# Attention beside a gated feed-forward layer: value products of two chunks together, row maxima eight blocks ahead, one ring of queries and keys

## The chip, the cores and the metric

The kernel runs on one core of a Trainium2 chip. A core has five engines, each with an instruction queue of its own that is worked through in order: PE (matmuls, with its weight loads shown as PEld), DVE (vector), ACT (scalar: exponentials, copies, casts), POOL (general purpose) and SP, which here issues nearly all DMA transfers. The metric is the device time of one execution in microseconds (us). Before the change it is 826.45 us, the median of 3 runs (826.08 to 826.83).

## The reference

Input x has 2048 rows of 512. The output is `g * a + (1 - g) * b` with `g = sigmoid(sum(x * gate_w))` per row. `b` is a feed-forward layer, `(silu(x @ w_gate) * (x @ w_up)) @ w_down` with 1792 hidden columns. `a` is attention with 32 heads of 16 columns and a window of 256:

```python
scores = jnp.einsum("bhqd,bhkd->bhqk", q, k) * (Dh ** -0.5)
mask = (idx[:, None] - idx[None, :] >= 0) & (idx[:, None] - idx[None, :] < W)
p = _softmax(jnp.where(mask[None, None], scores, -1e9), axis=-1)
o = jnp.einsum("bhqk,bhkd->bhqd", p, v)
```

All of it is float32. The kernel gets near that with a fast matmul type (F32R) by splitting each operand into a high and a low part, with three products (high-high, high-low, low-high) in place of one.

## The kernel before

**Blocks, chunks, groups.** The 2048 rows are 16 blocks of 128, or 4 chunks of 512. Eight groups `g` have four heads each; a group's heads are worked on as two pairs (`pr`), and the two heads of a pair lie in the lower and upper 64 partitions of one tile.

**Queries and keys.** `proj` or, in the main loop, a unit `("p", g)` computes a group's queries and keys. ACT copies the result out of PSUM, ACT casts the high part and POOL subtracts for the low part (`split_qk`, whose subtraction stands on the helper's line 68), into a tile pair `X`. Then `stack` (lines 242 to 248) writes rows of X into the tiles `QT` and `KT`: for each pair and each of three combinations of high and low parts one DMA for the queries and one for the keys, 12 in all, from SBUF to SBUF. A call moves half a sequence (1024 columns, 128 KB a DMA). There are two sets of QT and KT (`QT[g % 2]`): one group's scores are computed from one set while the next group's fill the other.

**Stage 1, stage 2, value products.** `stage1` (line 251) multiplies a block of queries with up to three blocks of keys on PE (line 263), and DVE adds the mask and takes each row's maximum (line 265). `put_max` (line 272) turns a half's maxima on DVE and writes them to DRAM in one DMA; `get_max` (line 278) brings them back in four DMAs as row 63 or 127 of the query tiles. The keys hold -1 there, so the second product comes out with the maximum taken off. `stage2` (line 293) computes the transposed scores on PE (line 304), ACT takes exponentials into tiles `pt` (line 306), and POOL zeroes what the window leaves out (lines 308, 311). `av` (line 316) multiplies a chunk's `pt` with the values, which `load_v` (line 288) has brought from DRAM: 96 matmuls (64 for chunk 0) in 64-by-32 tiles of the array (line 328), against 64-by-128 tiles everywhere else in the main loop. One PSUM bank of pool `pp` and one of `ps2` hold the two halves of the sum. `finish` (line 333) adds the halves, normalizes and sends the chunk to DRAM in five steps, with a DMA on POOL's queue.

**The main loop** (line 601) has 128 slots `t` (group `t // 16`, block `t % 16`) and one more. A slot has four steps (`hd` in the code). Each step puts into PE's queue one stage-1 product of the next group, one stage-2 product of this group and six matmuls of a unit (line 215). A unit takes four slots: the product of x with a 128-column part of a feed-forward weight (kept in DRAM as `raws`, lines 519 and 522) or the queries and keys of a later group. In the last group there is no stage 1. In the first of every four slots (`part == 0`), at step 1, one `av` follows, then `finish` begins. `later(t, hd, ...)` sets other work to a slot and step: `prepare` in step 3 of a unit's first slot splits the next weight (ACT, then POOL on line 68) and lets SP fetch the one after it (line 73). There is one buffer for a raw weight, so that fetch waits in SP's queue until POOL has read the last one. Nothing plans the order: each engine's queue is what the code writes, and SP's queue stands still behind a DMA that waits.

**Ahead of the loop**, x and the first weights are split, four value blocks and the first groups' queries and keys are computed, and stage 1 of group 0 (16 blocks) runs among the value products of the remaining blocks. **Behind it** comes the feed-forward part (`step`, `hidden`), whose first tiles come from `raws`, and the attention's output product.

Of the kernel before, what the change touches and what calls it, by code (L numbers as in the profile page):

```python
# [9 lines left out]
F32 = mybir.dt.float32  # L10
# [6 lines left out]
P = 128  # L17
# [11 lines left out]
EV = 5  # L29
# [4 lines left out]
def gated_mix(ctx, tc, xT, xn, w01, wqk, wv, wo, wgu, wd, gw, out):  # L34
# [14 lines left out]
    mxd = dram.tile([2 * G, P, 32], F32, name="mxd")  # L49
# [57 lines left out]
    QT = [[slot(f"q0{pr}") for pr in range(2)]]  # L107
    KT = [[slot(f"k0{pr}") for pr in range(2)]]
# [26 lines left out]
    for g in range(2, G):  # L135
        UNITS += early[:2] + [("p", g)] + early[2:3]
        early = early[3:]
# [20 lines left out]
    def load_wd(f, piece, raw=None, engs=dve):  # L158

        WD[f] = halves_of(piece)  # L160
        raw = fetch(wd[f], raw)
        return lambda: split(*WD[f], raw, *engs)
# [6 lines left out]
    with ExitStack() as A:  # L169
# [14 lines left out]
        def x_pair(pool=None, name="x"):  # L184
            return tuple((pool or sm).tile([P, 2 * CH], F32R, name=f"{name}{w}", bufs=1) for w in ("hi", "lo"))

        def split_qk(g, hf, cc, raw, los=nc.gpsimd):
            hi, lo = (t[:, cc * CH:(cc + 1) * CH] for t in X[g, hf])
            split(hi, lo, raw, nc.scalar, los)
# [40 lines left out]
        def proj(g, c, pool, name, todo=None, los=nc.gpsimd):  # L230

            hf, cc = divmod(c, 2)
            if cc == 0:
                X[g, hf] = x_pair() if g == hf else x_pair(vpool, f"x{g}{hf}")

            def done(ps):
                raw = kept()
                nc.scalar.copy(raw, ps)
                split_qk(g, hf, cc, raw, los)
# [10 lines left out]
        MX = {}  # L250
        def stage1(g, qb):

            hf, b = divmod(qb, NB // 2)
            if b == 0:
                MX[g, hf] = sm.tile([P, 4, NB // 2], F32, name="mx")
            q0, k0 = qb * P, max(0, qb - 2) * P
            n = q0 + P - k0
            for hd in range(4):
                pr, j = divmod(hd, 2)
                r = slice(64 * j, 64 * j + 63)  # L260

                ps = ps2.tile([P, CH], F32, name="ps2") if g == 0 and pr else ps1.tile([P, CH], F32, name="ps1")
                nc.tensor.matmul(ps[:, :n], QT[g % 2][pr][r, q0:q0 + P], KT[g % 2][pr][r, k0:k0 + n],  # L263
                                 start=True, stop=True)
                mx = nc.vector.tensor_tensor_reduce(out=ps[:, :n], in0=ps[:, :n], in1=mask[:, 3 * P - n:],  # L265
                                                    scale=1.0, scalar=NEG, op0=ALU.add, op1=ALU.max,
                                                    accum_out=MX[g, hf][:, hd, b:b + 1])
                if g == 0:
                    BEHIND.append(mx)
                yield  # L270

        def put_max(g, hf):
            mt = sm.tile([P, 32], F32, name="mt")
            nc.vector.transpose(mt, MX[g, hf].rearrange("p h b -> p (h b)"))
            u = 2 * g + hf
            nc.sync.dma_start(mxd[u], mt)

        def get_max(g, hf):
            v = mxd[2 * g + hf].rearrange("(q h b) e -> h b q e", q=4, h=4)
            for pr in range(2):  # L280
                q = halves_of(QT[g % 2][pr])[hf]
                for j in range(2):
                    nc.sync.dma_start(q[64 * j + 63:64 * j + 64].bitcast(F32).rearrange("p (b q e) -> p b q e", b=NB // 2, q=4),
# [9 lines left out]
        def stage2(g, kb):  # L293
# [4 lines left out]
            for hd in (1, 0, 3, 2):  # L298
# [4 lines left out]
                ps = ps1.tile([P, CH], F32, name="ps1") if g == G - 1 and pr else ps2.tile([P, CH], F32, name="ps2")  # L303
                nc.tensor.matmul(ps[:, :n], KT[g % 2][pr][r, k0:k0 + P], QT[g % 2][pr][r, k0:k0 + n],  # L304
# [11 lines left out]
        def av(g, c):  # L316


            AV[g, c] = (pp.tile([P, CH], F32, name="pb" if 4 * g + c + 1 < len(UNITS) else "pa"),
# [13 lines left out]
        def finish(g, c):  # L333


            first, second = AV[g, c]
            both = osb.tile([P, CH], F32, name="on")
            lo = 0 if c else 64
            nc.scalar.copy(both[:, lo:], second[:, lo:])
            yield  # L340
            nc.vector.tensor_tensor(out=both[:, lo:], in0=first[:, lo:], in1=both[:, lo:], op=ALU.add)
            if lo:
                nc.vector.tensor_copy(both[:, :lo], first[:, :lo])
            yield
            ot = osb.tile([P, CH], F32, name="on")
            nc.vector.transpose(ot, both)
            yield
            v = ot.rearrange("p (s e) -> p s e", e=32)
            rc = osb.tile([P, CH // 32], F32, name="rc", bufs=1)
            nc.vector.reciprocal(rc, v[:, :, DH])  # L350
            nc.vector.tensor_tensor(out=v[:, :, :DH], in0=v[:, :, :DH],
                                    in1=rc[:, :, None].to_broadcast([P, CH // 32, DH]), op=ALU.mult)
            yield
            on = osb.tile([P, CH], F32, name="on")
            nc.vector.transpose(on, ot)
            nc.gpsimd.dma_start(od[g, :, c * CH:(c + 1) * CH], on)
            yield
# [19 lines left out]

        fill_rows(QT[0], 0.0, 0, nc.vector)

# [35 lines left out]
        xraw = [h for w in "qk" for pr in range(2) for h in halves_of(slot(f"{w}1{pr}", F32))]  # L415
        xraw = [halves_of(h) for h in xraw]
        xraw = [[xraw[2 * c + k // 2][k % 2] for k in range(NK)] for c in range(NCH)]
# [27 lines left out]
        fill_rows(KT[0], -1.0, 0, nc.gpsimd)  # L445
        make_mask()
        split_w(0, nc.vector)
# [4 lines left out]
        fill_rows(QT[0], 0.0, 1, nc.gpsimd)  # L452
        fill_rows(KT[0], -1.0, 1, nc.gpsimd)
        run(vproj(0))
        split_x(1, range(2, NK))
        run(vproj(1))
        split_x(2, range(2))
        run(vproj(2))
        split_x(2, range(2, NK))
        run(proj(0, 1, pp, "pa", los=nc.vector))  # L460
        stack(0, 0)
        run(vproj(3))
        run(proj(1, 1, pp, "pa"))
        split_x(3)
        QT.append([slot(f"q1{pr}") for pr in range(2)])
        KT.append([slot(f"k1{pr}") for pr in range(2)])
        for c in range(2, NCH):
            run(proj(0, c, pp, "pa", los=nc.vector))
        for hf in range(2):
            fill_rows(QT[1], 0.0, hf, nc.gpsimd)  # L470
            fill_rows(KT[1], -1.0, hf, nc.gpsimd)
        stack(0, 1)
        send_v(1)
        send_v(3)
        stack(1, 0)


        first = chain(*(stage1(0, b) for b in range(NB)))
# [5 lines left out]
        for n, turn in enumerate(turns):  # L484
            for m, _ in enumerate(turn, 3 * NK * n):
                run(first, 2 * (2 * NB * max(m + 1 - 8, 0) // (total - 8) - 2 * NB * max(m - 8, 0) // (total - 8)))
            if n == 3:
                prepare()
            if n == 8:
                put_max(0, 0)  # L490
            if n == 9:
                get_max(0, 0)
        run(first)
        for c in range(2, NCH):
# [5 lines left out]
        ptp = A.enter_context(tc.tile_pool(name="ptp", bufs=13))  # L500
        osb = A.enter_context(tc.tile_pool(name="osb", bufs=2))
# [7 lines left out]
        def unit(key, t):  # L509
# [4 lines left out]
            def done(hf):  # L514
                def copies(ps):
                    t0 = t + 3 + hf
                    places = [kept(), kept()]
                    for m in range(2):
                        later(t0, 2 * m, lambda m=m: nc.scalar.copy(places[m], ps[m]))  # L519
# [296 lines left out]
```

## Time and profile before

| | |
|---|---|
| median of 3 runs | 826.45 us (826.08 to 826.83) |
| profiled execution, its own time | 825.82 us |
| its span, first to last instruction | 824.1 us |
| granted PE clock, share of full | 0.999 |
| busy: PE / PEld / DVE / ACT / POOL | 99% / 82% / 62% / 55% / 42% |
| mean DMA rate | 162 GB/s |
| DMAs that SP issues for `stack` / `put_max` / `get_max` | 192 / 16 / 64 |

The profile is of one execution, 0.63 us under the median of the runs; the span leaves out 1.7 us of it. PE is called busy while any matmul is in flight, so its 99% doesn't say that it runs at its best rate: the start times of its matmuls say that. In a timeline row stand the start, the time taken, engine, line, operation, output and inputs with their shape, and in brackets the idle time before it and what ended that. SPq is the queue of SP. "x2" joins two instructions.

### The profile page before, as it was taken

To read this page: it belongs to the slowest core of one execution; us is meant where nothing else is said; L and a number is where in the kernel's file an instruction comes from. 1 tells how busy PE (TensorE), PEld (TensorE's weight loads), DVE (VectorE), ACT (ScalarE), POOL (GpSimd) and SP (SyncE) were. 2 spreads that over 40 slices of the span, in tenths; PEclk is the share of its full clock that TensorE was granted. 3 is DMA by queue.
4 is the path that set the end of the run, shared out by engine and by line. 5 is a ranking of instruction groups with operands and counts; after the bars stand their busy time and mean duration, and the time that the engine had idled before them with its cause. 6 is when DMAs were issued, how large, how long until landed. Compare 5 with 4: busy or idle time off the path is not lost.

```text
span 824.1 us, 21565 instructions
## 1 busy us (share of the span) xinstructions
PE 815.9 (99%) x8306; PEld 677.6 (82%) x8306; DVE 509.8 (62%) x1422; ACT 451.6 (55%) x940; POOL 343.1 (42%) x631
## 2 busy tenths in 40 slices
PE   9999999999999999999999999999999999999998
PEld 6788988888888988887888888877778888888886
DVE  5496677677667676676677677745548443443443
ACT  6422666666666666666666666666647423334341
POOL 5812555555546555555554654456600111011020
PEclk9999999999999999999999999999999999999999
DMA  8484525625634643642652553556769444573621
GB/s 293 111 259 148 167 101 156 180 96 139 195 109 115 188 135 98 183 143 90 181 167 88 172 157 114 147 190 226 248 224 371 158 156 123 165 218 102 213 94 51
DMA packets 70582, 133.27 MB, mean 162 GB/s; under 512 B 14288, under 2 KB 19024, under 8 KB 70480
## 3 DMA queue, kind: packets, MB, share of 16 engines
q1 hardware_dynamic: 66512, 118.00, 46.4%
q0 software_dynamic: 3968, 13.90, 4.6%
q8 instruction: 65, 1.06, 0.5%
q14 instruction: 37, 0.30, 0.1%
HBM read 61.08 MB, written 45.61 MB: 129 GB/s over the span
## 4 chain that ended last, share of the span: by engine, by line
PE 88%; DMA 4%; POOL 3%; DVE 2%; SPq 1%; ACT 1%; issue 1%; ACTq 0%; POOLq 0%
PE pb L215 22%; PE pa L215 22%; PE pb L328 7%; PE ps L263 6%; PE ps L85 6%; PE ps L84 6%; PE ps L83 6%; PE ps L304 4%; PE pb L84 2%; PE pb L85 2%; PE pb L83 2%; PE ps L328 2%; DMA ev<-wd 1%; PE pb L708 1%; PE pa L708 1%
## 5 line engine op out<-in xcount | busy, mean ns | idle before, releaser
L265 DVE CUSTOM_DVE_ANT_0 ps<-ps,mask 128x384 f32<-128x384 f32 (+2 forms) x512 | 272.2, 540 | 142.5 <-PE ps L263 76.8
L306 ACT ACTIVATE pt<-ps 128x384 f32<-128x384 f32 (+2 forms) x512 | 240.8, 477 | 114.9 <-PE ps L263 56.8
L308 POOL TENSOR_SCALAR_AFFINE_SELECT pt<-pt 128x256 f32<-128x256 f32 x256 | 108.2, 423 | 212.5 <-ACT pt L306 204.0
L304 PE MATMUL ps<-q,k 64*128 64x384 f32 (+2 forms) x512 | 162.5, 328 | 0.0
L263 PE MATMUL ps<-k,q 63*128 63x384 f32 (+2 forms) x512 | 158.6, 330 | 0.0
L215 PE MATMUL pb<-xhi,wh 64*128 64x512 f32 x512 | 115.2, 394 | 0.0
L215 PE MATMUL pb<-xlo,wh 64*128 64x512 f32 x512 | 114.0, 391 | 0.0
L215 PE MATMUL pb<-xhi,wl 64*128 64x512 f32 x512 | 113.8, 392 | 0.0
L215 PE MATMUL pa<-xhi,wh 64*128 64x512 f32 x512 | 112.3, 393 | 0.0
L215 PE MATMUL pa<-xlo,wh 64*128 64x512 f32 x512 | 110.9, 391 | 0.0
L215 PE MATMUL pa<-xhi,wl 64*128 64x512 f32 x512 | 110.7, 391 | 0.0
L263 PEld LDWEIGHTS ps<-k,q 63*128 63x128 f32 x512 | 88.8, 185 | 16.1 <-issue 5.4
L311 POOL TENSOR_SCALAR_AFFINE_SELECT pt<-pt 128x256 f32<-128x256 f32 x224 | 98.7, 441 | 0.0
L304 PEld LDWEIGHTS ps<-q,k 64*128 64x128 f32 x512 | 93.0, 185 | 5.6 <-issue 0.8
L712 DVE TENSOR_TENSOR sg<-got,sg 128x512 f32<-128x512 f32 x50 | 44.5, 889 | 51.4 <-ACT sg L711 48.1
L328 PE MATMUL ps<-pt,vg 64*32 64x320 f32 (+4 forms) x1408 | 75.2, 346 | 0.0
L328 PE MATMUL pb<-pt,vg 64*32 64x320 f32 (+3 forms) x1360 | 74.0, 350 | 0.8 <-ACT ev L519 0.7
L265 DVE DVE_READ_ACCUMULATOR2_ANT mx<- 128x1 f32 x512 | 72.1, 141 | 0.0
L328 PEld LDWEIGHTS pb<-pt,vg 64*32 64x32 f32 x1360 | 46.5, 106 | 29.1 <-ACT pt L306 9.9
L215 PEld LDWEIGHTS pb<-xhi,wh 64*128 64x128 f32 x512 | 59.3, 185 | 8.6 <-ACT ev L519 0.3
L215 PEld LDWEIGHTS pb<-xhi,wl 64*128 64x128 f32 x512 | 59.3, 184 | 7.5
L215 PEld LDWEIGHTS pa<-xhi,wl 64*128 64x128 f32 x512 | 56.7, 184 | 7.9
(162 smaller groups left out, 1557.8 us busy)
## 6 DMA issues: line engine op xcount, KB each, us to landing
raws<-ev SPq DMA_DIRECT2D x104, 256.0 KB
got<-raws SPq DMA_DIRECT2D x100, 256.0 KB
od<-on POOLq DMA_DIRECT2D x32, 256.0 KB, 3.1
raw<-wgu SPq DMA_DIRECT2D x28, 256.0 KB
q<-xhi SPq DMA_DIRECT2D x56, 128.0 KB
k<-xhi SPq DMA_DIRECT2D x56, 128.0 KB
vd<-vs POOLq DMA_DIRECT2D x8, 672.0 KB, 5.9
vg<-vd SPq DMA_DIRECT2D x32, 168.0 KB
```

Source lines behind the costliest of these rows:

```text
L83: nc.tensor.matmul(ps, lh, rh, start=start and i == 0, stop=False)
L84: nc.tensor.matmul(ps, lh, rl, start=False, stop=False)
L85: nc.tensor.matmul(ps, ll, rh, start=False, stop=stop and i == n - 1)
L215: mm = nc.tensor.matmul(ps[me], w[r], x[r], start=not second and i == 0, stop=bool(second) and i == n - 1)
L263: nc.tensor.matmul(ps[:, :n], QT[g % 2][pr][r, q0:q0 + P], KT[g % 2][pr][r, k0:k0 + n], start=True, stop=True)
L265: mx = nc.vector.tensor_tensor_reduce(out=ps[:, :n], in0=ps[:, :n], in1=mask[:, 3 * P - n:], scale=1.0, scalar=NEG, op0=ALU.add, op1=ALU.m ...
L304: nc.tensor.matmul(ps[:, :n], KT[g % 2][pr][r, k0:k0 + P], QT[g % 2][pr][r, k0:k0 + n], start=True, stop=True)
L306: BEHIND.append(nc.scalar.activation(pt[:, j, :n], ps[:, :n], AF.Exp, scale=SCALE))
L308: nc.gpsimd.affine_select(out=pt[:, :, :P], in_=pt[:, :, :P], pattern=[[0, 2], [1, P]], compare_op=ALU.is_ge, fill=0.0, base=0, channel_mu ...
L311: nc.gpsimd.affine_select(out=pt[:, :, 2 * P:], in_=pt[:, :, 2 * P:], pattern=[[0, 2], [-1, P]], compare_op=ALU.is_ge, fill=0.0, base=-1, ...
L328: nc.tensor.matmul(AV[g, c][h][32 * j:32 * j + 32, q0 - c * CH:q1 - c * CH], VG[4 * g + kb // 4][o, kb % 4, 17 * j:17 * j + 32], PT[g, kb, ...
L712: nc.vector.tensor_tensor(out=sg, in0=gu[1], in1=sg, op=ALU.mult)
```

## The change

- **Value products of two chunks together.** `av` is called for two chunks one after the other in every eighth slot, in place of one chunk in every fourth. `finish` works on both. Both buffers of `ps2` and of the `pp` name are taken at once; `pt` has 21 buffers in place of 13, the tiles of `finish` 3 in place of 2.
- **Maxima eight blocks ahead.** Stage 1 in slot `t` is now for block `t + 8` of the whole run of 128 (`LAG`), across the border of groups, in place of the next group (16 ahead). Eight blocks of group 0 come ahead of the loop in place of 16, and the last eight slots have no stage 1 in place of the last 16. Maxima are put and fetched for four blocks at a time in place of eight: `put_max(u)` in step 0 and `get_max(u)` in step 3 of slot `4u - 4`.
- **One ring.** There is one set of QT and KT. A quarter of the columns is overwritten as soon as the old group is through with it: `stack(u)` at slot `4u - 11`, 12 DMAs for 512 columns (64 KB each), four calls a group in place of two.
- **X by quarters.** X pairs have 512 columns and come from a pool of five. A projection's result is split in the slot after it is copied, in steps 1 and 3; both PSUM copies now stand in steps 0 and 1 and the two `raws` DMAs in steps 2 and 3 of one slot. The query units move from the third to the fourth place of every four units.
- **What goes with it.** Raw x has tiles of its own at the start; group 1's projection of chunk 1 moves behind the value products; value blocks are loaded in every fourth slot, two slots ahead of the second chunk that needs them, in place of four or more. Seven down-projection weights are split in the last group's slots in place of nine, seven behind in place of five. `kept()` has six buffers in place of five, and the descriptor scratch of POOL's DMAs is set to 4096 bytes.

```diff
-        def stack(g, hf):
+        def quarter(t, c):
+            return t[:, c * CH:(c + 1) * CH]
+
+        def stack(g, c):
             for pr in range(2):
-                q, k = (halves_of(t[g % 2][pr])[hf] for t in (QT, KT))
-                hi, lo = (x[32 * pr:] for x in X[g, hf])
+                q, k = quarter(QT[pr], c), quarter(KT[pr], c)
+                hi, lo = (x[32 * pr:] for x in X[g, c])
...
-        def put_max(g, hf):
+        def put_max(u):
             mt = sm.tile([P, 32], F32, name="mt")
-            nc.vector.transpose(mt, MX[g, hf].rearrange("p h b -> p (h b)"))
-            u = 2 * g + hf
+            nc.vector.transpose(mt, MX[u % 2])
             nc.sync.dma_start(mxd[u], mt)
...
-        def finish(g, c):
...
+        def finish(g, hf):
+
+            cs = 2 * hf, 2 * hf + 1
+            both, ot, v = {}, {}, {}
+            for c in cs:
+                both[c] = osb.tile([P, CH], F32, name="on")
+                lo = 0 if c else 64
+                nc.scalar.copy(both[c][:, lo:], AV[g, c][1][:, lo:])
             yield
+            for c in cs:
+                lo = 0 if c else 64
+                nc.vector.tensor_tensor(out=both[c][:, lo:], in0=AV[g, c][0][:, lo:], in1=both[c][:, lo:], op=ALU.add)
...
-        first = chain(*(stage1(0, b) for b in range(NB)))
+        first = chain(*(stage1(b, ((ps1, "ps1"), (ps2, "ps2"))) for b in range(LAG)))
...
+        put_max(1)
+        for c in range(1, NCH):
             run(proj(1, c, pp, "pb"))
-        stack(1, 1)
-        for n in range(4):
-            load_v(n)
+        get_max(1)
...
-                        later(t0, 2 * m, lambda m=m: nc.scalar.copy(places[m], ps[m]))
+                        later(t0, m, lambda m=m: nc.scalar.copy(places[m], ps[m]))
...
-                            later(t0 + m, 2 - 2 * m, lambda m=m: nc.sync.dma_start(raws[key[1], key[2], 2 * hf + m], places[m]))
+                            later(t0, 2 + m, lambda m=m: nc.sync.dma_start(raws[key[1], key[2], 2 * hf + m], places[m]))
...
-                    t1 = t0 + 3 * hf
-                    later(t1, 3, lambda: half(0))
-                    later(t1 + 1, 1, lambda: half(1))
-                    later(t1 + 1, 3, lambda: stack(g, hf))
+                    for m in range(2):
+                        later(t0 + 1, 1 + 2 * m, lambda m=m: half(2 * hf + m, m))
...
+        for u in range(4, 4 * G):
+            later(4 * u - 11, 0, lambda u=u: stack(*divmod(u, 4)))
+        for u in range(2, 4 * G):
+            later(4 * u - 4, 0, lambda u=u: put_max(u))
+            later(4 * u - 4, 3, lambda u=u: get_max(u))
...
-            s1 = stage1(g + 1, i) if t < g7 else iter(())
+            s1 = stage1(t + LAG, ((ps1, "ps1"),) * 2) if t + LAG < G * NB else iter(())
...
-                if hd == 1 and part == 0:
-                    while tops:
-                        top = tops.pop()
-                        put_max(*top)
-                        later(t + 1, 1, lambda top=top: get_max(*top))
-                    if t:
-                        ag, c = divmod(d - 1, NCH)
+                if hd == 1 and t % 8 == 0 and t:
+                    ag, hf = divmod(t // 8 - 1, 2)
+                    for c in (2 * hf, 2 * hf + 1):
                         av(ag, c)
-                        FIN = finish(ag, c)
-                        run(FIN, 1)
-            if i in (7, 15) and g + 1 < G:
-                tops.append((g + 1, i // 8))
-            if t >= 10 and t % 4 == 2 and t + 6 < G * NB:
-                load_v((t + 6) // 4)
+                    FIN = finish(ag, hf)
+                    run(FIN, 2)
+            if t % 4 == 2 and t < G * NB:
+                load_v(t // 4)
```

More of the change, by code (lines that the diff above doesn't have):

```diff
@@ L105, in halves_of @@
         return [t[:, :n], t[:, n:]]
-    QT = [[slot(f"q0{pr}") for pr in range(2)]]
-    KT = [[slot(f"k0{pr}") for pr in range(2)]]
+    QT = [slot(f"q{pr}") for pr in range(2)]
+    KT = [slot(f"k{pr}") for pr in range(2)]
+    xq = ctx.enter_context(tc.tile_pool(name="xq", bufs=5))
     WT = {}
@@ L182, in gated_mix, with x_pair, split_qk @@
         X = {}
[L184 to L189, printed above, removed]
+        def x_pair():
+            return tuple(xq.tile([P, CH], F32R, name=f"x{w}") for w in ("hi", "lo"))
+        def split_qk(g, c, raw, los=nc.gpsimd):
+            split(*X[g, c], raw, nc.scalar, los)
         def whole(pool, name, todo, done):
@@ L248, in stack, with stage1 @@
                     nc.sync.dma_start(k[b::4].bitcast(F32), kx[64:96].bitcast(F32))
[L250 to L255, printed above, removed]
+        MX = [sm.tile([P, 32], F32, name=f"mx{i}", bufs=1) for i in range(2)]
+        def stage1(s, pools):
+            u, b = divmod(s, 4)
+            qb = s % NB
             q0, k0 = qb * P, max(0, qb - 2) * P
@@ L302, in stage2 @@
                     pt = PT[g, kb, pr] = ptp.tile([P, 2, 3 * P], F32, name="pt")
-                ps = ps1.tile([P, CH], F32, name="ps1") if g == G - 1 and pr else ps2.tile([P, CH], F32, name="ps2")
-                nc.tensor.matmul(ps[:, :n], KT[g % 2][pr][r, k0:k0 + P], QT[g % 2][pr][r, k0:k0 + n],
+                late = g * NB + kb >= G * NB - LAG and pr
+                ps = ps1.tile([P, CH], F32, name="ps1") if late else ps2.tile([P, CH], F32, name="ps2")
+                nc.tensor.matmul(ps[:, :n], KT[pr][r, k0:k0 + P], QT[pr][r, k0:k0 + n],
                                  start=True, stop=True)
@@ L456, in gated_mix @@
         run(vproj(1))
+        run(proj(0, 1, pp, "pa", los=nc.vector))
+        stack(0, 1)
         split_x(2, range(2))
         run(vproj(2))
+        fill_rows(QT, 0.0, 1, nc.gpsimd)
+        fill_rows(KT, -1.0, 1, nc.gpsimd)
         split_x(2, range(2, NK))
-        run(proj(0, 1, pp, "pa", los=nc.vector))
-        stack(0, 0)
         run(vproj(3))
[L463 to L472, printed above, removed]
         send_v(1)
         send_v(3)
-        stack(1, 0)
-        first = chain(*(stage1(0, b) for b in range(NB)))
+        split_x(3)
+        for c in (2, 3):
+            run(proj(0, c, pp, "pa", los=nc.vector))
+            stack(0, c)
+        first = chain(*(stage1(b, ((ps1, "ps1"), (ps2, "ps2"))) for b in range(LAG)))
         turns = []
@@ L543, in gate_place @@
         def gate_place():
[L544 to L545 removed]
+            XG.extend(h.bitcast(F32) for _ in range(2) for h in x_pair())
             nc.sync.dma_start(XG[0], gw[None, :].to_broadcast([P, D]))
@@ L614, in gated_mix @@
                 run(turns[part], 3)
-                if (part, hd) in ((0, 2), (1, 1), (2, 1), (3, 1)):
+                if t % 8 == 0 and hd in (2, 3) or t % 8 and hd == 1:
                     run(FIN, 1)
@@ L721, in gated_mix @@
         ACC = {}
-        GA = by_k(slot("k11", F32))
+        GA = wop.tile([P, NK, D], F32, name="ga")
+        for n in range(11, NF):
+            pieces.append([wop.tile([P, D], F32R, name=f"wd{n}{w}") for w in ("hi", "lo")])
         def block(b, c, n, hh, hl):
```

131 lines of the change are left out of this document (61 added, 70 removed).

## The prediction

> **What bounds the kernel now.** I read the page first, then PE's timeline around one value product, then SP's timeline and waits.
>
> ```profile
> span 824.1 us, 21565 instructions
> PE 815.9 (99%) x8306; PEld 677.6 (82%) x8306; DVE 509.8 (62%) x1422; ACT 451.6 (55%) x940; POOL 343.1 (42%) x631
> ```
>
> PE is the bound, and no other engine is near. Being busy isn't being at its best, so the starts count. In PE's timeline a step of a slot begins with a stage-1 or stage-2 product (L263, L304):
>
> ```profile
> 240.43 0.33 PE L304 MATMUL ps<-q,k 64*128 64x384 f32 x1
> ...
> 241.29 0.34 PE L263 MATMUL ps<-k,q 63*128 63x384 f32 x1
> ...
> 241.94 0.40 PE L215 MATMUL pa<-xhi,wl 64*128 64x512 f32 x2
> 242.26 0.45 PE L328 MATMUL pb<-pt,vg 64*32 64x320 f32 x1
> ...
> 244.23 0.27 PE L328 MATMUL pb<-pt,vg 64*32 64x128 f32 x1
> ...
> 244.42 0.30 PE L328 MATMUL ps<-pt,vg 64*32 64x128 f32 x2
> ...
> 244.75 0.44 PE L263 MATMUL ps<-k,q 63*128 63x384 f32 x1
> ...
> 245.50 0.40 PE L215 MATMUL pa<-xhi,wl 64*128 64x512 f32 x2
> 245.73 0.33 PE L304 MATMUL ps<-q,k 64*128 64x384 f32 x1
> ...
> 246.60 0.33 PE L263 MATMUL ps<-k,q 63*128 63x384 f32 x1
> ```
>
> A plain step takes 0.87 us (245.73 to 246.60; 240.43 to 241.29 is 0.86), a slot without values 3.48. The step with a value product takes 3.46, and the one behind it 0.98. So a chunk costs 3.46 - 0.87 + 0.98 - 0.87 = 2.70 us, and not all of that is value matmuls. SP has much slack, but this change nearly doubles its work, so it is the queue to follow. Its timeline, with the chain's transfer rows and the durations of one line:
>
> ```profile
> 64.94 0.34 SPq L276 DMA_DIRECT2D mxd<-mt  x1
> 68.13 2.95 SPq L283 DMA_DIRECT2D q<-mxd  x4
> ...
> 81.01 0.53 SPq L247 DMA_DIRECT2D q<-xhi  x1
> ...
> 87.98 0.59 SPq L248 DMA_DIRECT2D k<-xhi  x1
> ...
> 91.97 0.38 SPq L276 DMA_DIRECT2D mxd<-mt  x1
> ...
> 94.47 2.87 SPq L283 DMA_DIRECT2D q<-mxd  x4
> 97.43 0.86 SPq L522 DMA_DIRECT2D raws<-ev  x2
> ```
>
> ```profile
> 259.37 0.53 SPq L247 DMA_DIRECT2D q<-xhi  x1
> ...
> 266.86 0.59 SPq L248 DMA_DIRECT2D k<-xhi  x1
> ```
>
> ```profile
> 28.54 2.44 DMA k<-xlo
> ...
> 562.63 3.32 DMA ev<-wd
> ```
>
> ```profile
> L283 SPq DMA_DIRECT2D q<-mxd x64: 649/654/1784, 68.1 to 546.5; - x64
> ```
>
> The twelve issues of a `stack` spread over 6.97 us (81.01 to 87.98) or 7.49 (259.37 to 266.86) from first to last. One lands 2.44 us after its issue begins; a 256 KB load takes 3.32. From a put of maxima to the first fetch that needs it pass 2.50 (91.97 to 94.47) to 3.19 us (64.94 to 68.13); four fetches take 2.9.
>
> **The change part by part.**
>
> *Two chunks together: -5.9 us.* The matmuls stay. What falls away, 16 times, is one entry into the value products and one exit. Entry: matmul pairs start 0.23 us apart (245.50 to 245.73), but the first value matmul comes 0.32 behind the last pair (241.94 to 242.26): 0.09. Exit: the last eight value matmuls begin at 244.42 and the next step at 244.75, 0.33 later, while they themselves began 0.19 behind the eight before them (244.23). A chunk that followed would begin 0.13 to 0.19 behind them by that, so 0.14 to 0.20 is saved. The step behind takes 0.98 in place of 0.87: 0.11. Together 0.34 to 0.40, I take 0.37; 16 x 0.37 = 5.9 (5.4 to 6.4). If the second chunk must wait, this is given back there, which I count below. The two `ps2` banks are no new wait: the first chunk's is copied out by ACT while PE works on the second, and the second's as today.
>
> *Start and end: -2.3 us.* PE waited once for the split of the last chunk of x:
>
> ```profile
> 31.68 0.39 PE L195 MATMUL pa<-xhi,wh 128*128 128x512 f32 x1
> 32.39 0.50 PE L195 MATMUL pa<-xlo,wh 128*128 128x512 f32 x1 [0.32 <-DVE xlo L68]
> ```
>
> That start is 0.71 after the one before it, 0.48 more than 0.23. Group 1's projection is moved away in front, so PE comes there 12 matmuls (2.7) earlier; but its copy and cast stood ahead of that split on ACT and go too. I take the 0.5 as gained (0.5 lost to 0.5 gained). Two late value products wait for PSUM copies that wait for buffers:
>
> ```profile
> 566.97 0.39 PE L215 MATMUL pa<-xhi,wl 64*128 64x512 f32 x1
> 567.81 0.45 PE L328 MATMUL pb<-pt,vg 64*32 64x320 f32 x1 [0.45 <-ACT ev L519]
> ```
>
> Here 0.84 in place of 0.32; the one at 583.73 lost 0.36 in the same way. With a sixth buffer, and two places for value products in place of four in the last group, I take 0.9 (0 to 0.9). At the start of the feed-forward part PE waits for tiles from `raws`:
>
> ```profile
> 595.48 10.59 SPq L522 DMA_DIRECT2D raws<-ev  x4
> ...
> 607.78 3.91 SPq L697 DMA_DIRECT2D got<-raws  x8
> ```
>
> ```profile
> 610.63 0.39 PE L85 MATMUL ps<-q,k 128*128 128x512 f32 x1
> 611.80 0.50 PE L83 MATMUL ps<-q,hh 128*128 128x512 f32 x1 [0.78 <-ACT hh L65]
> ```
>
> It lost 1.17 - 0.23 = 0.94. SP can fetch only behind the last `raws` (595.48 + 10.59), whose copy now stands a step earlier. Against it work DVE's double `finish` and two more weight loads; I take 0.9 (0 to 0.9).
>
> *Half as long transfers, twice as many: +14.7 us.* `stack` has 384 DMAs in place of 192, the gets 128 in place of 64, the puts 32 in place of 16. All stand on SP, and no row shows a 64 KB transfer of this kind. Bounds: the issue as for 128 KB (0.64 apart, 6.97/11) or less with the size, down to the 0.43 of `raws`. The 4 KB fetches of maxima take 0.65 each (row L283 above), so size doesn't set it; I take 0.64. Landing: 2.44.
>
> The Trainium skill (DMA: Bandwidth & Descriptors, section Rules for kernel authors) speaks against this part: transfers under 64 KB pay mostly overhead, and many small ones should be made one. By it, too, the halved transfers would gain nothing on the old ones, and the sum would stay as it is with 0.64.
>
> Now the place. In slots 8k the value pair stands in step 1, and `prepare` in step 3. SP's fetch waits there for POOL, and the 12 DMAs of the next slot's `stack` stand behind it:
>
> ```profile
> 229.11 0.34 PE L263 MATMUL ps<-k,q 63*128 63x384 f32 x1
> ...
> 230.99 1.30 POOL L68 TENSOR_TENSOR wl<-raw,wh 128x512 fp32r<-128x512 f32 x1
> ...
> 232.31 0.33 SPq L73 DMA_DIRECT2D raw<-wgu  x1
> ```
>
> ```profile
> SPq L73 <- POOL wl L68: 87.4, 17, 6.1
> ```
>
> Step 3 begins at 229.11 (call it H), the fetch is issued at H + 3.2. In slots 16m (m = 1 to 6) the second half of X is split in the same step ahead of it, another POOL subtraction of 1.3 us (the row at 230.99 is of that kind): H + 4.5. The transfers are needed by stage 1 three slots later (slot 8k + 4), the second pair's six in step 2: H + 0.87 + 3 x 3.48 + 2 x 0.87 = H + 13.05. The last one lands at fetch + 0.4 + 6.97 + 2.44: H + 13.0 in slots 16m + 8, H + 14.3 in slots 16m. With 7.49 add 0.5. So PE waits 1.3 us (0.9 to 1.8) six times, 7.8, and 0.25 (0 to 0.5) eight times, 2.0.
>
> What is late next: let S be the issue of that last transfer, PE going on at S + 2.44. SP then issues the values of slot 8k + 2 (0.4, as a `raws`) and two `raws` (0.9), then the put at S + 2.0, waits 2.5 to 3.2 for it, fetches (2.9), a `raws` and the weight (0.8), and 12 transfers (7.6): S + 15.8 to 16.5, then the values for slot 8k + 8, landing 2.4 to 3.3 later, S + 18.2 to 19.8. PE needs them for its second chunk at S + 2.44 + 2 x 0.87 + 3 x 3.48 + 2 x 0.87, and the first chunk, 1.8 us where it is chunk 0: S + 18.2. It waits 0 to 1.6, I take 0.7, in seven groups: 4.9. The maxima are needed in slot 16m + 6 at S + 2.44 + 5.2 = S + 7.7 and land at S + 2.0 + 2.85 + 0.7 + 2.4 = S + 8.0; a wait there comes off the later one.
>
> *At nothing:* DVE's `finish` for two chunks bunches up behind the pair. Its rows:
>
> ```profile
> L265 DVE CUSTOM_DVE_ANT_0 ps<-ps,mask 128x384 f32<-128x384 f32 x112 | 62.5, 562 | 29.1 <-PE ps L304 16.3 <-PE ps L263 12.1
> L346 DVE STREAM_TRANSPOSE on<-on 128x512 f32<-128x512 f32 x8 | 5.7, 707 | 0.0
> ```
>
> Two maxima and two such operations are 2.5 us in two steps of 0.98 + 0.87: 0.7 late. The second buffer of `ps1` covers a step; without it 16 x 0.7 = 11. The moved copies, the sixth buffer and POOL's smaller descriptor scratch cost nothing: ACT and POOL are at 55% and 42%, and the fills of the second ring, which fall away, stood on POOL.
>
> Sum: -5.9 - 0.5 - 0.9 - 0.9 + 7.8 + 2.0 + 4.9 = +6.5. The profiled execution took 825.82, so 832.3; the median stands 0.6 above it: **832.9 us**.
>
> **The rivals.**
>
> *SP keeps up.* If issuing half the bytes takes 0.5 us in place of 0.64, the twelve end 1.5 us earlier and all waits but about one microsecond go: 826.45 - 8.2 + 1 = 819. For it: the issues are 0.53 when the queue has been empty (81.01, 259.37). Against it: 0.65 for 4 KB. The Trainium skill (the same page, section Issuing engines are not separate DMA queues) says that issue time is usually small beside the transfer; by that this rival would hold, while the rows have 12 issues of 7 us beside a landing of 2.44.
>
> *Waits and gain cancel.* With 6.97 and the early landings throughout: 6 x 0.9 + 0 + 7 x 0.3 = 7.5 against 8.2: 825.7.
>
> *SP becomes the bound of the whole loop, clearly slower.* In 16 slots it issues 48 transfers (7.49 + 0.59 for 12, so 32.3), 16 fetches (11.5), 12 `raws` (5.2) and 12 single ones (4.4), 53.4 us, and stands 4 x 2.4 behind its puts and some 5 us behind the fetch of slot 16m: 68.0. PE takes 65.37 for them now, the same value product coming again at
>
> ```profile
> 307.63 0.45 PE L328 MATMUL pb<-pt,vg 64*32 64x320 f32 x1
> ```
>
> (242.26 to 307.63), and 64.6 with two merges. The 3.4 more in each of seven groups decide from the point where the puts take 3.2 us each time and the twelve 7.5: 826.45 - 8.2 + 24 = 842, and up to 850 if the twelve take 8.5.
>
> **How the numbers follow.** Forecast 0.40, SP keeps up 0.29, cancel 0.14, SP bound 0.17. Its own range is 828 to 839 (the waits at their ends). Within 0.2% (824.8 to 828.1) is what a measurement can't tell from no change. Faster 0.29, same 0.14, slower 0.57. The range 817 to 846 takes in both sides.
>
> **What would show it.** Right: value products of 192 and 160 matmuls without a break in every eighth slot, steps 0.87; PE's waits in slots 16m + 4, step 2, for `stack`'s DMAs (L263), 1 to 2 us each, and at second chunks for `vg`; SP with hardly a pause in 65 us; groups 66 to 68 us long. Wrong: twelve issues in under 6 us, no such waits, groups of 64.5. If DVE or ACT ended PE's waits in the loop, the cause would be another one.

## The result: 7.5% slower, and the profile after

The changed kernel takes 887.52 us (median of 4 runs, 885.50 to 890.27) against 826.27 for the kernel before beside it. The ratio is 1.0749, 95% interval 1.0713 to 1.0784. The forecast, 832.9 us with a range from 817 to 846, had the sign and missed the size by 55 us.

The head of the page of the changed kernel (its profiled execution took 888.04 us):

```profile
span 886.3 us, 22139 instructions
PE 829.2 (94%) x8306; PEld 702.5 (79%) x8306; DVE 514.0 (58%) x1438; ACT 458.3 (52%) x942; POOL 333.2 (38%) x623
```

PE has as many matmuls as before and is no longer busy all the time. Where the 62.2 us of span lie is read from the starts of groups 1 and 7 and of slot 15 of group 7, in PE's timeline of the kernel before:

```profile
142.73 0.33 PE L304 MATMUL ps<-q,k 64*128 64x384 f32 x1
...
534.75 0.34 PE L304 MATMUL ps<-q,k 64*128 64x384 f32 x2
...
594.03 0.22 PE L304 MATMUL ps<-q,k 64*128 64x128 f32 x1
```

and of the changed one:

```profile
138.95 0.44 PE L304 MATMUL ps<-q,k 64*128 64x384 f32 x1
...
565.36 0.44 PE L304 MATMUL ps<-q,k 64*128 64x384 f32 x1
...
648.23 0.22 PE L304 MATMUL ps<-q,k 64*128 64x128 f32 x1
```

| stretch | before | after | difference |
|---|---|---|---|
| up to group 1 | 142.7 | 139.0 | -3.8 |
| groups 1 to 6 | 392.0 | 426.4 | +34.4 |
| last group, 15 slots | 59.3 | 82.9 | +23.6 |
| from there to the end | 230.1 | 238.1 | +8.0 |

Eight slots of stage 1 moved from the first stretch to the third. By an estimate that is 2.8 us each way: a step of PE takes 0.87 us with a stage-1 product and 0.78 without in the kernel before, so 0.35 a slot.

**In the loop** PE waits for the transfers of `stack` (k) and for values (vg). The view of PE's waits from 138 to 565 us (total, times, longest):

```profile
PE ps L264 <- DMA k<-xhi: 11.9, 10, 1.8
PE pb L327 <- DMA vg<-vd: 6.8, 7, 2.8
PE ps L264 <- DVE on L355: 4.9, 5, 1.3
PE ps L304 <- DMA q<-mxd: 3.4, 3, 2.5
```

One of them, in slot 4 of group 2, as the prediction walked it. PE's timeline has step 3 of slot 0, which the prediction calls H, at 217.61:

```profile
217.61 0.33 PE L304 MATMUL ps<-q,k 64*128 64x384 f32 x1
...
230.43 0.40 PE L216 MATMUL pa<-xhi,wl 64*128 64x512 f32 x2
232.38 0.41 PE L264 MATMUL ps<-k,q 63*128 63x384 f32 x1 [1.55 <-DMA k<-xhi]
```

SP's timeline has the fetch and the twelve transfers behind it:

```profile
221.96 0.33 SPq L74 DMA_DIRECT2D raw<-wgu  x1
222.40 0.53 SPq L248 DMA_DIRECT2D q<-xhi  x1
...
229.62 0.59 SPq L249 DMA_DIRECT2D k<-xhi  x1
```

The fetch goes out at H + 4.35 (forecast 4.5), the last transfer is issued at 229.62, and PE starts 2.76 later, with a gap of 1.95 where 0.23 is plain: 1.7 us lost (forecast 1.3, 0.9 to 1.8). The view of SP's waits for the whole of group 2 (209.41 to 279.92, 70.5 us):

```profile
SPq L282 <- DMA mxd<-mt: 7.7, 4, 3.0
SPq L74 <- POOL wl L69: 6.6, 2, 5.0
SPq L248 <- PE ps L264: 2.2, 6, 0.8
SPq L519 <- ACT ev L516: 0.7, 2, 0.5
SPq L519 <- ACT pt L306: 0.5, 2, 0.4
SPq L519 <- ACT wh L66: 0.4, 1, 0.4
SPq L519 <- ACT on L339: 0.2, 1, 0.2
```

These are 18.3 us; in the other 52.2 SP issues. Such a sum always fills the group, so what matters is the kind of wait. 14.3 us come from SP's own order: it stands behind its own puts and, at the fetch, behind POOL. With the issues they make 66.5 us, more than the 64.5 that PE needs for a group without stops (run 3). Only the other 4.0 are waits for PE and ACT. So SP is taken to set the length of a group, 70.5 to 72.3 us in groups 1 to 6; runs 3 and 10 test that.

**In the last group** one stop is 10 us long. SP's timeline, then DVE's, then PE's, then PE's clock in the window behind the stop (the granted clock is the third number from the end):

```profile
583.73 0.54 SPq L248 DMA_DIRECT2D q<-xhi  x1
...
592.44 0.58 SPq L74 DMA_DIRECT2D ev<-wd  x1
```

```profile
595.25 0.43 DVE L68 CAST xhi<-ev 128x512 fp32r<-128x512 f32 x1 [9.33 <-DMA ev<-wd]
```

```profile
586.78 0.54 PE L216 MATMUL pb<-xhi,wl 64*128 64x512 f32 x2
597.00 0.69 PE L264 MATMUL ps<-k,q 63*128 63x384 f32 x1 [9.68 <-DVE mx L265]
...
597.48 0.63 PE L216 MATMUL pb<-xhi,wh 64*128 64x512 f32 x2
597.91 0.63 PE L216 MATMUL pb<-xlo,wh 64*128 64x512 f32 x2
```

```profile
598.00:603.00 5.00, 5.00 (x28) 4.15 (x26) 3.40 (x11) 2.15 (x6) 2.52 (x5) 0.50 0.69 233
```

The first down-projection weight stands in SP's queue behind the last twelve transfers. DVE's split of it stands in DVE's queue ahead of the maxima, so PE gets no PSUM bank for stage 1. Then PE works at least 5 us at half clock (pairs 0.43 apart in place of 0.23).

### The profile page after: what moved, and what is told of

It reads as the page before. It is cut to its first block, busy times and chain, and to the rows that moved or that the text cites. A ratio compares the mean times of both kernels' runs of the same rounds, so it can differ in the third digit from the quotient of the medians.

```text
span 886.3 us, 22139 instructions
## 1 busy us (share of the span) xinstructions
PE 829.2 (94%) x8306; PEld 702.5 (79%) x8306; DVE 514.0 (58%) x1438; ACT 458.3 (52%) x942; POOL 333.2 (38%) x623
## 4 chain that ended last, share of the span: by engine, by line
PE 75%; DMA 10%; SPq 8%; DVE 3%; issue 2%; ACT 1%; POOL 1%; DVEq 0%; POOLq 0%
PE pa L216 16%; PE pb L216 16%; PE ps L84 6%; PE ps L85 6%; PE ps L86 6%; PE ps L264 5%; PE pb L327 4%; SPq L249 4%; DMA vg<-vd 3%; PE ps L304 3%; SPq L248 3%; PE pb L196 2%; PE ps L327 2%; PE pa L196 2%; PE pb L85 2%
## 5 line engine op out<-in xcount | busy, mean ns | idle before, releaser
L264 PE MATMUL ps<-k,q 63*128 63x384 f32 (+2 forms) x512 | 165.7, 333 | 31.0 <-DMA k<-xhi 12.5
L304 PE MATMUL ps<-q,k 64*128 64x384 f32 (+2 forms) x512 | 167.0, 333 | 5.0 <-DMA q<-mxd 5.0
L264 PEld LDWEIGHTS ps<-k,q 63*128 63x128 f32 x512 | 92.5, 186 | 51.2 <-DVE mx L265 19.1
L216 PE MATMUL pb<-xhi,wh 64*128 64x512 f32 x512 | 111.5, 397 | 0.0
L216 PE MATMUL pb<-xlo,wh 64*128 64x512 f32 x512 | 110.2, 394 | 0.0
L216 PE MATMUL pb<-xhi,wl 64*128 64x512 f32 x512 | 110.2, 394 | 0.0
L327 PE MATMUL pb<-pt,vg 64*32 64x320 f32 (+4 forms) x1312 | 73.3, 361 | 9.9 <-DMA vg<-vd 9.1
L327 PE MATMUL ps<-pt,vg 64*32 64x320 f32 (+4 forms) x1408 | 77.8, 356 | 0.0
L327 PEld LDWEIGHTS pb<-pt,vg 64*32 64x32 f32 x1312 | 49.5, 109 | 31.6 <-issue 9.6
L216 PEld LDWEIGHTS pa<-xhi,wh 64*128 64x128 f32 x512 | 57.8, 187 | 4.3
```

What stands on the lines that cost most here:

```text
L216: mm = nc.tensor.matmul(ps[me], w[r], x[r], start=not second and i == 0, stop=bool(second) and i == n - 1)
L264: nc.tensor.matmul(ps[:, :n], QT[pr][r, q0:q0 + P], KT[pr][r, k0:k0 + n], start=True, stop=True)
L304: nc.tensor.matmul(ps[:, :n], KT[pr][r, k0:k0 + P], QT[pr][r, k0:k0 + n], start=True, stop=True)
L327: nc.tensor.matmul(AV[g, c][h][32 * j:32 * j + 32, q0 - c * CH:q1 - c * CH], VG[4 * g + kb // 4][o, kb % 4, 17 * j:17 * j + 32], PT[g, kb, ...
```

## The experiments

Ratios are to the kernel before, with 95% intervals; groups are measured from start to start.

**1. The fetch behind `stack`.**

```diff
-        PEND.pop(0)()
-        prefetch()
+        PEND.pop(0)()
...
             later(t, 3, prepare)
+            later(t + 1, 0, prefetch)
```

> The changed kernel with one thing moved: the fetch of the next raw weight stands in SP's queue behind the twelve transfers of stack, in place of ahead of them. Theory A (SP's queue in order is the bound: in a group of 16 slots it issues for 55.8 us and stands 8.0 us behind its puts and 6.7 behind that fetch, together the 70.5 us that a group takes): the 6.7 go, SP needs about 64 us a group, PE is the bound again or nearly, groups take 65 to 66.5 us and the kernel 845 to 862 us. Theory B (SP has time, but the halved transfers land late because of their number or bytes on the DMA engines): the order changes little, 880 to 890 us. Theory C (the pair of value products or the bunched work of DVE and ACT sets the waits): no change, 883 to 890 us.

Measured 875.29 us (1.0602, 1.0581 to 1.0623). The waits for k in slots 4 and 12 are gone, groups take 66.9 to 69.6 us. But PE's waits show a new one in their place:

```profile
PE pb L326 <- DMA vg<-vd: 12.3, 10, 1.8
```

So the fetch was one cause, but most of what it gave was lost at the next thing that SP brings: groups 1 to 6 got 13.8 us shorter together, where SP's waits for the fetch had been 6.6 us in group 2 alone. Theories B and C don't allow the gain; A had priced it too high. SP's waits in group 2 (206.83 to 275.67, 68.84 us) begin with

```profile
SPq L281 <- DMA mxd<-mt: 8.4, 4, 2.5
SPq L274 <- DVE mt L273: 2.8, 2, 1.9
```

and are 17.0 us in all, so SP issues for 51.8 us. With the 8.4 behind its own puts that is 60.2 us, less than PE's 64.5, and still the group takes 68.8. The place counts too. By the code the kernel before issues a chunk's values ten slots ahead of their product, the changed kernel those of a pair's second chunk only two slots ahead and directly behind twelve transfers.

**2 and 3. Half the bytes, half the number.** In `stack`: only the first half of each transfer's columns, or six of its twelve transfers.

```diff
-                    nc.sync.dma_start(q[b::4].bitcast(F32), qx[:32].bitcast(F32))
+                    nc.sync.dma_start(halves_of(q[b::4].bitcast(F32))[0], halves_of(qx[:32].bitcast(F32))[0])
```

> The changed kernel, whose stack issues as many transfers but moves only the first half of the columns of each (32 KB in place of 64; the other half of the scores is left wrong). Theory A: the issues take as long, so 882 to 889 us and groups of 70 to 72 us. Theory B: transfers land sooner, PE's waits for k and q shrink by half or more, below 870 us. Theory C: no change, 883 to 890.

```diff
-                    nc.sync.dma_start(q[b::4].bitcast(F32), qx[:32].bitcast(F32))
-                    nc.sync.dma_start(k[b::4].bitcast(F32), kx[64:96].bitcast(F32))
+                    if b == 0 or b == 1 + pr or g == 0:
+                        nc.sync.dma_start(q[b::4].bitcast(F32), qx[:32].bitcast(F32))
+                    if b == 2 - pr or g == 0:
+                        nc.sync.dma_start(k[b::4].bitcast(F32), kx[64:96].bitcast(F32))
```

> The changed kernel, whose stack issues six of its twelve 64 KB transfers in the loop (the others are left out, so scores are wrong). Theory A: SP issues 15.3 us less a group, 55 us in all, PE is the bound, groups of 64.6 to 65.5 us, and the last group gets shorter too, 835 to 852 us. Theory B: half the bytes and half the number, much the same gain as with half the bytes alone. Theory C: no change, 883 to 890.

Half the bytes: 885.71 us (one run). The issues of 32 KB in its SP timeline, twelve in 6.96 us as for 64 and 128 KB:

```profile
291.52 0.54 SPq L248 DMA_DIRECT2D q<-xhi  x1
...
298.48 0.59 SPq L249 DMA_DIRECT2D k<-xhi  x1
```

Half the number: 841.54 us (one run), and groups 3 to 6 take 64.53 us each, 0.80 under the 65.33 of before. It is the number of transfers, not the bytes; theory B is out. That the number counts by its issues in SP's queue, and not on the DMA engines, is shown by run 10, where every transfer of `stack` stays.

**4. The old kernel with doubled transfers.** Each of `stack`'s transfers in two halves, all else as before the change.

> The kernel before, whose stack is issued in twice as many transfers of half the size (64 KB, as in the changed kernel), all else as it was. Theory A: SP stood idle or waiting for 33 of 65 us in each group and nothing is needed soon, so 826 us, within 0.3%. Theory B: the small transfers cost PE time by themselves, over 835 us.

Measured 864.34 us (1.0479, 1.0458 to 1.0500). Theory A's "no change" was wrong by 38 us: SP waited or stood idle for about half the time, and that was no reserve at the place where it was needed. Runs 12 and 15 look for the reason.

**5 to 8. Each cure alone, then all four.** Two rows of maxima in one DMA; values loaded in pairs at slots 8k + 2 (on top of run 1); the first two late weights earlier and the fetches of maxima ahead of the gate's; everything.

```diff
-                for j in range(2):
-                    nc.sync.dma_start(q[64 * j + 63:64 * j + 64].bitcast(F32).rearrange("p (b q e) -> p b q e", b=4, q=4),
-                                      v[2 * pr + j:2 * pr + j + 1])
+                nc.sync.dma_start(q[63::64].bitcast(F32).rearrange("p (b q e) -> p b q e", b=4, q=4), v[2 * pr:2 * pr + 2])
...
-            if t % 4 == 2 and t < G * NB:
+            if t % 8 == 2 and t < G * NB:
                 load_v(t // 4)
+                load_v(t // 4 + 1)
...
-        for m, t in enumerate((1, 3, 5, 9, 10, 11, 13)):
+        for m, t in enumerate((-2, 0, 5, 9, 10, 11, 13)):
```

> The changed kernel, whose get_max fetches the rows 63 and 127 of a query tile in one DMA: two issues in place of four each time, eight fewer in a group. Theory A (SP's queue, in order, sets the length of a group): SP saves 8 x 0.65 = 5.1 us a group, the maxima land 1.3 us sooner, groups come to 65 to 67.5 us and the kernel to 850 to 868 us. Theory D (the bound is not SP's issue time but one late transfer a group, such as the values): 880 us or more.

> The kernel with the fetch behind stack (875 us), and besides the values of both chunks of a pair are loaded in slots 8k + 2, so the second chunk's four slots sooner. In that kernel PE lost 14.8 us in six groups at value products, and SP stood 1.9 to 2.9 us a group ahead of puts, which wait for PE's late scores. Theory A (SP would be fast enough, 56 us of issues and about 8 us behind its puts, if PE's waits did not hold its puts up): the waits for values go, groups 64.6 to 66.5 us, kernel 850 to 864 us. Theory A2 (SP has no reserve at all: what is won at the values is lost at the next wait, for keys or maxima): 868 to 877 us.

> The changed kernel with two things of the last group moved: the first two down-projection weights are loaded in slots g7 - 2 and g7, ahead of the last stack, in place of g7 + 1 and g7 + 3, and the four fetches of maxima stand in SP's queue ahead of the fetch for the gate, which waits for DVE. Theory E (PE's stop of about 10 us in slot 3 of the last group comes from that weight alone, whose load stands behind the twelve transfers of the last stack while DVE's queue waits for it ahead of the maxima): the stop goes, 870 to 879 us. Theory F (it is only SP's lateness from the loop, which will show at the next step whichever it is): 882 to 889 us.

> All four edits in the changed kernel: fetch behind stack, maxima in two fetches, values of both chunks early, first weights of the last group and the fetches of maxima ahead. Theory A: SP issues about 51 us a group and waits 8 to 9, PE is the bound again, groups 64.5 to 65 us as with half of stack left out, the last group 62 to 66 us, the kernel 817 to 830 us: at or below the kernel before. Theory A2: groups stay above 66 us, kernel above 838 us.

Two fetches: 869.35 us (1.0516, 1.0484 to 1.0547), groups 67 to 70.7, a little above theory A's ranges and far below D's. Values early: 871.11 (1.0552, 1.0523 to 1.0581): PE's waits for values fell from 12.3 us to none, those for keys and queries rose from 2.9 to 12.7, as theory A2 says of a queue without reserve:

```profile
PE ps L263 <- DMA k<-xhi: 12.7, 6, 3.0
```

Weights early: 883.28 (1.0686, 1.0649 to 1.0724); the 10 us stop went and PE stood idle for 5.9, 4.1 and 3.9 us in slots 0, 4 and 7 of that group; the first weight now stood behind the stack before. Theory F fits better than E. All four: 840.73 (1.0190, 1.0159 to 1.0221). The loop is cured (groups of 64.5 to 65.4 us), but the last group still took 76.1 us, so the time is above theory A's 817 to 830.

**10. The loop's three edits alone** (those of runs 1, 5 and 6, without the last group's).

> The changed kernel with the three edits of the loop alone. Theory A: groups 64.5 to 65.2 us; the last group and what follows as in the changed kernel, so 838 to 852 us. If SP were not the loop's bound, groups of 66 us or more.

Measured 840.53 us (1.0175, 1.0162 to 1.0188). Runs 1 and 5 gave 12 and 18 us singly, run 6 another 4 on top of run 1; the three together give 47. The last group's edit, which run 8 has besides, added nothing. From 136 to 524 us PE waited 1.0 us in all, and group 4 starts and ends, in PE's timeline, at

```profile
331.04 0.33 PE L301 MATMUL ps<-q,k 64*128 64x384 f32 x1
...
395.57 0.33 PE L301 MATMUL ps<-q,k 64*128 64x384 f32 x1
```

that is 64.53 us, with all 384 transfers in place. SP's waits in this group begin with

```profile
SPq L280 <- DMA mxd<-mt: 6.6, 4, 2.6
SPq L274 <- DVE mt L273: 4.4, 3, 1.9
```

and are 18.5 us in all, so it issues for 46.0; with the 6.6 behind its own puts that is 52.6 us. Now it is SP that waits for DVE's maxima and for ACT, and PE's waits went nearly all at once. Counted in the same way, run 6 had 63.6 us (53.0 of issues and 10.6 behind puts, group 3) and groups of 68.6 to 70.1. So a sum a little under PE's 64.5 (60.2 in run 1, 63.6 in run 6) didn't do, and 52.6 did; how much reserve is needed lies between and wasn't tried. Nor was another engine's queue for some of the transfers.

**9 and 11. The end cured, and with it single against paired.** Gate in slots g7 + 6 to g7 + 13, weights later with a longer lead; then the same with one chunk in every fourth slot, in `finish` too.

```diff
-            later(GATE0 + b, 3, lambda b=b: gate_block(b))
+            later(GATE0 + b // 2, 1 + 2 * (b % 2), lambda b=b: gate_block(b))
...
-            later(t, 2, lambda: later(t + 1, 2, load_wd(f, piece or x_pair(), kept())))
+            later(t, 2, lambda: later(t + 2, 2, load_wd(f, piece or x_pair(), kept())))
...
+        pre = {n: load_wd(ORDER[n + 5], pieces[n + 5], raw2(), (nc.scalar, nc.vector)) for n in (2, 3)}
         for _ in range(3):
             load_kept(*loads.pop(0))
```

> The changed kernel with the three edits of the loop (fetch behind stack, maxima in two fetches, values of both chunks early), and besides for its end: the gate's 16 blocks run in slots g7 + 6 to g7 + 13, two a slot, in place of one a slot from g7 - 2; no down-projection weight is loaded ahead of slot g7 + 3 and each has two slots in place of one until DVE splits it; the first two weights behind the loop are loaded ahead of the first six tiles from raws. Theory G (the stops of the last group come from DVE's queue waiting for a weight that stands behind stack in SP's queue, and from SP's fetches for the gate that wait for DVE): groups 64.5 us, the last group's 15 slots 62 to 66 us in place of 76 to 83, the rest 230 to 233, the kernel 818 to 828 us. Theory H (one ring leaves no room for more than seven early weights, and the feed-forward part loses 6 us or more at its start whatever the order): 828 to 838 us.

> The kernel with the edits of loop and end, but one chunk's value products in every fourth slot, as before the change. By the prediction's term of 0.37 us for each entry and exit saved, 16 of them, it takes 5 to 7 us more than with two chunks together, and a group 65.2 to 65.4 us. If pairs save nothing, within 1.5 us of it.

Paired 827.88 us (1.0034, 1.0017 to 1.0051), single 833.26 (1.0086, 1.0073 to 1.0099): 5.4 us. That difference holds more than merges: the single kernel's last group is 6.5 us longer and what follows it 6.9 shorter. The groups before are the cleaner measure. Group 5 in the timelines, paired (64.53) and single (65.36):

```profile
394.80 0.33 PE L301 MATMUL ps<-q,k 64*128 64x384 f32 x1
...
459.33 0.33 PE L301 MATMUL ps<-q,k 64*128 64x384 f32 x1
```

```profile
400.99 0.33 PE L301 MATMUL ps<-q,k 64*128 64x384 f32 x1
...
466.35 0.33 PE L301 MATMUL ps<-q,k 64*128 64x384 f32 x1
```

Two merges save 0.83 us, 0.41 each. In the paired kernel the last group took 62.2 us, as theory G has it, but the rest took 238.3 where G has 230 to 233, and PE stopped 6.1 us behind the last value products: the gate ended late, and SP's fetches for the feed-forward part stood behind it.

**12 and 15. Why doubling hurt the old kernel.** The second twelve of each 24 two slots later; or the second half of X split two slots later.

> The kernel before with twice as many transfers of half the size, as in the earlier run of 864 us, but the second twelve of each 24 issued two slots later. Theory J (in that run it was the burst of 16 us in SP's queue, behind which raws and maxima came late and held up PSUM copies): 825 to 832 us. Theory K (it is the number of issues in all, or the small transfers themselves): 850 us or more.

> The kernel before with twice as many transfers of half the size (864 us), whose second half of X is split two slots later. Theory L (there the 24 issues held the one pair of X tiles too long: ACT stood up to 3.6 us behind the transfers that still read it, with the copies that PE's value products need behind it in its queue): PE's stops of 2.4 to 4.6 us at value products in slots 16m go, groups take 65.3 to 67 us, and the kernel 832 to 848 us, the rest being lost ahead of the loop. Theory K (the number of issues in itself): groups of 69 to 70 us and 858 us or more.

Spread: 865.22 us (1.0475, 1.0458 to 1.0493), no gain, so theory J falls; but two slots are 7 us and twelve issues 7.6, so the 24 still stood together. The trace shows another holder. In ACT's timeline, then PE's:

```profile
228.42 0.62 ACT L65 CAST xhi<-ev 128x512 fp32r<-128x512 f32 x1 [3.31 <-DMA k<-xhi]
```

```profile
229.95 0.74 PE L329 MATMUL pb<-pt,vg 64*32 64x320 f32 x1 [2.83 <-ACT ev L520]
```

ACT can't overwrite the one pair of X tiles while transfers read it, and the PSUM copy that PE needs stands behind that cast. With X split later (852.93 us; 1.0327, 1.0302 to 1.0352) these stops at value products go, and 11 us with them; groups of 66.6 to 69.0 remain, where ACT now waits for `raws` transfers (14.4 us in 12 waits). So the X pair is shown for a part; which share is the number of issues in itself stays open, as does the 10 us lost ahead of the loop.

**13, 16 and 17. Three orders of the gate** in run 9's kernel: one block a slot from g7 - 2; six from g7 + 2 and ten at two a slot; five from g7 - 2, a pause from g7 + 3, and eleven 0.75 to 1 slot apart.

> As the kernel with the edits of loop and end (827.9 us), but the gate's blocks stay where the changed kernel has them, one a slot from g7 - 2, with the fetches of maxima ahead of the gate's fetch in SP's queue. In that kernel PE stopped 6.1 us behind the last value products: the last gate block came late, SP's fetches for the feed-forward part stood behind it, and ACT's PSUM copies behind those. If that is all that is left, the stop falls to 3 us or less, the last group stays at 62 to 64 us, and the kernel takes 819 to 825 us, faster than the kernel before. If one ring with seven early weights costs 6 us at the start of the feed-forward part in any order, 826 to 832 us.

> As the kernel with the edits of loop and end, with the gate's blocks between the two places tried: six of them one a slot from g7 + 2, ten two a slot in g7 + 8 to g7 + 12, and the last early weight a slot sooner. With the gate from g7 - 2 PE stopped 5.7 us in slot 4 of the last group and hardly at the start of the feed-forward part (231.9 us from there to the end); with the gate in g7 + 6 to g7 + 13 it was the other way round (62.2 us for 15 slots, then a stop of 6.1). If both are queue order, this order has neither: 15 slots in 62 to 64 us, 232 to 234 behind them, the kernel 819 to 824 us, faster than the kernel before by 0.3 to 0.8%. If the loss only moves about, as the two tried so far would have it, 826 to 829 us.

> As the kernel with the old gate (827.3 us), where PE's stop of 5.7 us in slot 4 of the last group had this cause: the gate's sixth block stood in DVE's queue ahead of the maxima and waited 6.1 us for its rows, whose fetch stood behind the twelve transfers of the last stack. Here the gate pauses from g7 + 3 to g7 + 5, and the other eleven blocks follow 0.75 to 1 slot apart until g7 + 13; the last early weight comes a slot sooner. If the rest of the loss is queue order: 15 slots of the last group in 62 to 64 us, 231 to 233 us behind them, the kernel 819 to 823 us, faster than before the change. If the gate's chain of two buffers (fetch, then block) can't go faster than a block in 2.7 us: a stop of 2 to 6 us near slot 13 or at the start of the feed-forward part again, 824 to 828 us.

None reached the time that it was built for (819 to 825, 824 and 823 us); each came out in the range of its rival. The first: 827.26 us (1.0021, 1.0011 to 1.0030); hardly anything was lost at the feed-forward part (231.9 us from there to the end), but PE stood idle for 5.6 us in slot 4, for a cause that its DVE timeline names:

```profile
551.26 0.69 DVE L544 SCALAR_TENSOR_TENSOR xlo<-xlo,xhi 128x512 f32<-128x512 f32 x1 [6.07 <-DMA xlo<-xn]
```

The second: 828.07 (1.0031, 1.0011 to 1.0051), with stops of 1.4 us in slot 5, 2.6 in slot 13 and 1.2 at the feed-forward part: the loss moved about. The third: 824.81 (0.9988, 0.9975 to 1.0001), which can't be told from the kernel before. Its last group took 64.5 us and the rest 232.3; stops of 1.2 and 2.8 us in slots 4 and 5 stay.

## Why the prediction was wrong in size

- *Two chunks together, -5.9:* right. 0.41 us a merge in group 5 of runs 9 and 11, where 0.37 was forecast, and 5.4 between the two kernels. In the changed kernel itself part of it was given back, as allowed for, where the second chunk waited.
- *The issue 0.64 apart whatever the size; fetch, transfers and need in slots 16m:* right, with 1.7 us in the slot shown.
- *What is late next:* this step failed. Lateness was followed through one pass, as if SP started each group on time, and the waits came to 14.7 us, about 2 a group. The rival "SP becomes the bound of the whole loop", given 0.17, is what happened in the loop, though its own time, 842 to 850 us, was far too low as well. Its sum was 68.0 us a group, measured 70.5 to 72.3. Its issues (53.4) were right within 1.2 us; its waits (14.6) were too few. They were 18.3 in group 2: 7.7 behind the puts in place of 9.6, 6.6 behind the fetch in place of 5, and 4.0 of small waits that had no term. The loop's cost, counted with the saved merges (0.8 a group), was 39 us where the sum had 14.7 for the whole run. Runs 3 and 10 show it by cure: with SP's own path well under PE's 64.5 us a group the waits go together, and cures taken singly pass the lateness on (runs 1 and 6).
- *Start and end, -2.3:* the start held (3.8 us earlier, of which an estimated 2.8 is moved work). At the end a gain was booked for fewer late value products and for copies a step earlier, and nothing for what stands behind the last `stack` in SP's queue. Weights, gate rows and values stand there, and DVE waits for them ahead of the maxima. Measured are 23.6 and 8.0 us more, of which 2.8 is moved work, beside 34.4 in the loop. With the loop alone cured (run 10) 16.9 and 6.3 remain. That queue order is the cause is shown by runs 9, 13 and 17, which then take most of that away by order alone. Run 17 still has 2.4 us (5.2 less the moved 2.8) and 2.2 us more than before in these two stretches; that they would go too is not shown. So the change as a whole can be brought level with the kernel before, and no run made it faster.
- *DVE's double `finish` at nothing:* in the changed kernel PE waits 4.9 us at "DVE on L355", a line of `finish`. Run 10 has the same `finish`, and none of that wait: PE's 1.0 us there is at other places. So it costs PE nothing where SP isn't late.
- *SP keeps up, 0.29:* the rival needed shorter issues for half the bytes, and run 2 shows them the same for 32 KB as for 64 and 128. The Trainium skill (DMA: Bandwidth & Descriptors, section Issuing engines are not separate DMA queues) calls issue time usually small beside the transfer. One issue of 0.59 us stands beside a landing of 2.5, but twelve in one queue take 7 us, and the rival resting on it fell. The Trainium skill (the same page, section Rules for kernel authors) says that many small transfers should be made one; the runs agree, by number: half the bytes changed 887.5 to 885.7 us, half the number to 841.5.

## What to carry to other kernels

Write down an in-order DMA queue over a whole period, its issues and the waits that come from its own order, and compare the sum with the bound engine's period. Above it, each group starts as late as the last ended, and a cure for one wait feeds the next. Well below it, lateness was made up here (52.6 beside 64.5 us); a little below it, it was not (60.2 and 63.6). Nor does idle time on average help: the old kernel's SP issued for only half the time, and doubled transfers still cost 38 us, in part because they held the one pair of X tiles longer. Before a burst is put into such a queue, list what stands behind it and which engine waits for that in its own order (here a weight and DVE), above all where the loop ends.

## What the hardware showed besides

A short stop can cost PE more than its length. The gap ahead of 162.19 in the changed kernel was 1.81 us of idleness, and the clock then stood at half for 3 us (PE's timeline, then the window behind it):

```profile
162.19 0.41 PE L264 MATMUL ps<-k,q 63*128 63x384 f32 x1 [1.81 <-DMA k<-xhi]
```

```profile
163.00:166.00 3.00, 3.00 (x18) 2.85 (x16) 1.30 (x5) 1.50 (x4) 1.29 (x3) 0.50 0.33 107
```

Stops of 2.29, 2.78, 3.90 and 9.68 us (ahead of 572.14, 392.10, 672.99 and 597.00) were followed by half clock too, but stops of 2.17 and 2.50 us (ahead of 617.77 and 310.36) left it at 1.00. So the length alone doesn't decide. Summed over windows of 1 us, PE's busy time times the missing share of the clock is 10.4 us in the changed kernel and 0.0 in the kernel before. The Trainium skill (TensorE: Matmul & The Clock Gate, Part 1: The HAM clock gate) has the clock halved after an idle window of about 3.4 us that runs freely; the free window fits that a longer stop passed and a shorter one didn't, but 1.81 us is well under its length.
